# Attention and two gated layers on one core: where the softmax sums of a pair of heads are inverted

## Chip, core and metric

One core of a Trainium2 chip runs the whole program. The metric is device time in microseconds (us), taken on the chip. The kernel before was run three times: 758.63, 758.64 and 758.89 us, median 758.64 us.

## What is computed

The inputs are `q`, `k`, `v` of 2 batches x 8 heads x 1152 positions x 64, and the weights of two gated layers on 1152 tokens of width 512 with 1536 hidden units.

```python
q_pool = q.reshape(B, H, S // 2, 2, D).mean(axis=3)
scores = np.matmul(q_pool, k.transpose(0, 1, 3, 2)) / np.sqrt(D)
attn = np.exp(scores - np.max(scores, axis=-1, keepdims=True))
attn = attn / (np.sum(attn, axis=-1, keepdims=True) + 1e-09)
x = np.matmul(attn, v)                     # then heads side by side: 1152 x 512
xn = x / np.sqrt(np.mean(x * x, -1) + 1e-6) * rms_g
y = (silu(xn @ w_gate) * (xn @ w_val)) @ w_out
out = (sigmoid(y @ w_gate2) * (y @ w_val2)) @ w_out2
```

The part that matters here is the division by the sum of the exponentials plus 1e-9. There are 576 pooled queries per head, so 576 sums per head.

## The kernel before

**Heads in pairs.** The 16 heads are worked through as 8 pairs. Of each head the 576 queries are five chunks of columns (`QCOL`): chunk 0 has 64 queries, chunks 1 to 4 have 128 each. From pair 1 on, chunk 0 of both heads is one block of 128 rows. The scores of a chunk (`s`) come in three matmul groups of 384 keys; VectorE (DVE) copies each out of PSUM with its running maximum (`e,m<-s`), makes the negated maximum `nb` of the three, and ScalarE (ACT) takes the exponential of the chunk, which writes the sum of each row into a column of `sums`. The tensor engine (PE) then transposes the exponentials (`eT`), 128 keys at a time.

**High and low parts.** Each fp32 operand of a product is split into a rounded high part and the rest. For the transposed exponentials `et` ACT writes the high part out of PSUM (line 579) and DVE the low part (line 580). In some units (`POOL_UNITS`) ACT copies the block out (`er`, line 575) and GpSimd (POOL) does both parts (lines 142 and 143, in the function `split`). The products `o` with V follow at a lag of four slots for a DVE unit and of five for a POOL unit (`AV_LAG`).

**Slots.** The order of all engines is written out by hand: `at(g, rank, fn)` puts a step into slot `g`, and a slot's steps are issued by rank, then by the order in which they were registered. Each head has 18 slots: 0 to 8 for the first three query chunks, 9 to 17 for the last two. The scores of a pair begin 15 slots ahead of its first head's slots. Each engine works through its own queue in this order and never past an instruction that waits.

**What sits around the change.** The last exponential of the first head of a pair falls into slot 6 of that head, that of the second head 16 slots on. One slot behind each of them, four after the score unit, `recip` puts two instructions: POOL adds 1e-9 to that head's sums (line 528, 128x5), then DVE takes the reciprocal into `rc` (line 529). When both heads of a pair have their products, the sum `osb` is formed (lines 599, 600), and `o_step` turns it back: PE transposes it (`oT`, line 620), ACT copies it out (`os`, line 631), and POOL multiplies by `rc` (line 629), once for chunks 0 to 2 and once for chunks 3 and 4. The first of these comes some nine slots after the second head's sums.

**Other work in these slots.** POOL also splits the next pair's Q and K (`qq`, `kh`, `kl`) from ACT's copies `kqt`, and V (`vv`). PE transposes K (`kT`, line 339) into the same four PSUM banks (tag "t") that `eT`, `qT` and `oT` use. In the odd heads 1, 3, 5, 9, 11 and 13 a weight block is prepared piece by piece (`w_spread`): ACT lines 208, 216 and 250, DVE lines 228 and 235, POOL lines 236 and 251. After the attention come the two gated layers (lines 741, 840 and 869), which are dense matmuls.

Of the kernel before, what the change touches and what calls it, by code (L numbers as in the profile page):

```python
# [8 lines left out]
F32 = mybir.dt.float32  # L9
# [3 lines left out]
ALU = mybir.AluOpType  # L13
# [3 lines left out]
P = 128  # L17
# [43 lines left out]
def tile_attention_moe_moe(ctx, tc, q, k, v, w_gate1, w_val1, w_out1, rms_g, w_gate2, w_val2, w_out2, out):  # L61
# [3 lines left out]
    nc = tc.nc  # L65
# [13 lines left out]
    NQC = len(QCOL)  # L79
# [12 lines left out]
    def pool(name, side="left", **kw):  # L92
        p = tc.alloc_tile_pool(name=name, bufs=1, side=side, **kw)
        pools.append(p)
        return p
# [9 lines left out]
    ap = pool("ap")  # L105
    ae = pool("ae", side="right")
# [4 lines left out]
    def bank(tag, name):  # L111
        return ps.tile([P, 512], F32, tag=tag, bufs=NBANK[tag], name=name)
# [15 lines left out]
    def at(g, rank, fn):  # L128
        count[0] += 1
        agenda.setdefault(g, []).append((rank, count[0], fn))  # L130
# [163 lines left out]


    kk, qq, vv, esb, osb, tbank = {}, {}, {}, {}, {}, {}
    raw, rcp, xall, sums, eneg, oacc, kst = {}, {}, {}, {}, {}, {}, {}

    SCORES = [[(0, 3), (0, 4), (0, 1), (0, 2), (0, 0)] + [(1, 1), (1, 2), (1, 0), (1, 3), (1, 4)]]
    SCORES += (NP - 1) * [[(0, 1), (0, 2), (0, 0), (0, 3), (0, 4), (1, 1), (1, 2), (1, 3), (1, 4)]]  # L300
# [181 lines left out]
    def s_unit(g, p, k):  # L482

        n, u = divmod(k, NSU)
        j, c = SCORES[p][n]
        i = 2 * p + j
        both = c == 0 and p > 0
        if k == 0:  # L490
            for h in (i, i + 1):
                sums[h] = ap.tile([P, NQC], F32, tag="sums", bufs=4, name="sums")
                esb[h] = {}
                if p == 0:
                    nc.gpsimd.memset(sums[h][QH:P, 0:1], 1.0)
        if u == 0:
            e = ap.tile([P, NSU * SU], F32, tag="e", bufs=8, name="e")
            esb[i][c] = e, 0
            if both:
                esb[i + 1][c] = e, 1  # L500
            eneg[i, c] = (ap.tile([P, NSU], F32, tag="m", bufs=3, name="m"), ap.tile([P, 1], F32, tag="nb", bufs=3, name="nb"))
        e, _ = esb[i][c]
        m, nb = eneg[i, c]
        r = slice(0, P if c or both else QH)
        s = bank("s" if p or k % 4 < 2 else "o", "s")
        kc = slice(u * SU, (u + 1) * SU)
        if both:
            kh, kl = kst[p]
            products = ((qbd[:, 0], kh), (qbd[:, 0], kl), (qbd[:, 1], kh))
        else:  # L510
            products = [(qq[i][:, part, QCOL[c]:QCOL[c] + r.stop], kk[i]) for part in range(2)]
        for n1, (qs, ks) in enumerate(products):
            nc.tensor.matmul(s[r, 0:SU], qs, ks[:, kc], start=(n1 == 0), stop=(n1 == len(products) - 1))  # L513

        def top():

            nc.vector.tensor_scalar(e[r, kc], s[r, 0:SU], 1.0, None, op0=ALU.mult, op1=ALU.max, accum_out=m[r, u:u + 1])  # L517
            if u == NSU - 1:
                nc.vector.tensor_reduce(nb[r], m[r], op=ALU.max, axis=AX.X, negate=True)  # L519

        def swap():
            for h in range(2):
                nc.gpsimd.tensor_copy(sums[i + 1][h * QH:(h + 1) * QH, 0:1], sums[i][(1 - h) * QH:(2 - h) * QH, 0:1])

        def recip():
            if p not in rcp:
                rcp[p] = ae.tile([P, NQC, 2], F32, tag="rc", bufs=2, name="rc")
            nc.gpsimd.tensor_scalar(sums[i], sums[i], 1e-9, 1.0, op0=ALU.add, op1=ALU.mult)
            nc.vector.reciprocal(rcp[p][:, :, j], sums[i])

        at(g, 17, top)
        if u == NSU - 1:
            at(g + EXP_LAG, 12, lambda: nc.scalar.activation(e[r], e[r], AF.Exp, bias=nb[r], scale=1.0, accum_out=sums[i][r, c:c + 1]))  # L533
            if both:
                at(g + 4, 24, swap)
            if n in (4, len(SCORES[p]) - 1):
                at(g + 4, 25, recip)

    def part_of(i, j):
        part, kc = divmod(j, NK)  # L540
# [44 lines left out]
    def av_unit(g, i, part, kc, et):  # L585
        n = NB if part else NA
        if kc == 0:
            oacc[i, part] = bank("o", "o")
        o = oacc[i, part]
        for k in range(2):  # L590
            nc.tensor.matmul(o[:, 0:n], vv[i][:, kc, :], et[:, k, :], start=(kc == 0 and k == 0), stop=(kc == NK - 1 and k == 1))  # L591
        if kc == NK - 1:

            p, odd = divmod(i, 2)
            if p not in osb:
                osb[p] = ae.tile([P, SQ], F32, tag="osb", bufs=1, name="osb")
            r1, r2 = (LP, HP) if odd else (HP, LP)
            ob = osb[p][r1, part * NA:part * NA + n]
            at(g, 11, lambda: nc.scalar.activation(ob, o[r1, 0:n], AF.Copy))
            at(g, 18, lambda: nc.vector.tensor_tensor(ob, o[r2, 0:n], ob, op=ALU.add))  # L600
            g += 1 if i == NHEAD - 1 and part else 2
            if odd:
                at(g, 7, lambda: o_step(g, p, part))

    def o_step(g, p, part):

        b, hp = divmod(p, NPAIR)
        if b not in xall:
            if b == B - 1:
                xa = ae.tile([P, NCA, DM], F32, tag="xa", bufs=1, name="xa")  # L610
                xb = ae.tile([P, NQC - NCA, DM], F32, tag="xb", bufs=1, name="xb")
            else:

                xa, xb = [xpool.tile([P, NDM * (NT - NX0) // DM, DM], F32, tag=f"x{s}1", name="x") for s in "hl"]
            xall[b] = ((xa, 0, NCA), (xb, NCA, NQC))
        x, c0, c1 = xall[b][part]
        n = c1 - c0
        t = bank("t", "oT")
        for c in range(c0, c1):
            nc.tensor.transpose(t[:, (c - c0) * P:(c - c0 + 1) * P], osb[p][:, QCOL[c]:QCOL[c] + P], ident)  # L620
        os = ae.tile([P, 512], F32, tag="kqt", bufs=3, name="os").rearrange("p (c d) -> p c d", d=P)[:, 0:n]
        xs = x[:, 0:n, hp * P:(hp + 1) * P]

        def norm():
            def by_head(t):
                return t.rearrange("p c (j d) -> p c j d", j=2)

            r = rcp[p][:, c0:c1].rearrange("p c (j o) -> p c j o", o=1)
            nc.gpsimd.tensor_tensor(by_head(xs), by_head(os), r.to_broadcast([P, n, 2, D]), op=ALU.mult)

        at(g + 1, 14, lambda: nc.scalar.activation(os.rearrange("p c d -> p (c d)"), t[:, 0:n * P], AF.Copy))
        at(g + 1, 41, norm)
        if hp == NPAIR - 1:
            x_steps(g + 2, b, part)
# [73 lines left out]
    for p in range(NP):  # L708
        for n in range(len(SCORES[p]) * NSU):
            g = 2 * p * NJ + (S0 if p else S00) + n * 2 * NJ // (len(SCORES[p]) * NSU)  # L710
            at(g, 2, lambda g=g, p=p, n=n: s_unit(g, p, n))
    for i in range(NHEAD):
        p, odd = divmod(i, 2)
# [201 lines left out]
```

## Time and profile before

| | us |
|---|---|
| median of three runs | 758.64 |
| the profiled execution's own time | 758.52 |
| its span, first to last instruction | 756.7 |
| PE busy in the span | 733.5 |
| DVE busy | 466.1 |
| ACT busy | 434.8 |
| POOL busy | 396.5 |

The granted TensorE clock is 1.000 over the whole span, which is the 2.4 GHz level. Attention takes about the first 300 us, the gated layers the rest. Matmuls are pipelined, so a row of PE shows from the start of a matmul to its modelled end, and busy time of PE overstates how full it is: what counts is when the next one starts. "Idle before" is time in which an engine did nothing although its queue had work, with what ended it.

### The profile page before, as it was taken

To read this page: it belongs to the slowest core of one execution; us is meant where nothing else is said; L and a number is where in the kernel's file an instruction comes from. 1 tells how busy PE (TensorE), PEld (TensorE's weight loads), DVE (VectorE), ACT (ScalarE), POOL (GpSimd) and SP (SyncE) were. 2 spreads that over 40 slices of the span, in tenths; PEclk is the share of its full clock that TensorE was granted. 3 is DMA by queue.
4 is the path that set the end of the run, shared out by engine and by line. 5 is a ranking of instruction groups with operands and counts; after the bars stand their busy time and mean duration, and the time that the engine had idled before them with its cause. 6 is when DMAs were issued, how large, how long until landed. Compare 5 with 4: busy or idle time off the path is not lost.

```text
span 756.7 us, 12442 instructions
## 1 busy us (share of the span) xinstructions
PE 733.5 (97%) x4501; PEld 690.4 (91%) x4501; DVE 466.1 (62%) x1122; ACT 434.8 (57%) x870; POOL 396.5 (52%) x445
## 2 busy tenths in 40 slices
PE   8999999999999998999999999999999999999997
PEld 6788988888888888999999999999999999998886
DVE  7877878778787888788777664333264456543010
ACT  6787878787888875456555445432354455455000
POOL 6567768677868661166545347442253345347100
PEclk9999999999999999999999999999999999999999
DMA  8536382727273310033332224321222232222011
GB/s 228 132 77 155 82 183 62 182 49 187 63 173 76 95 44 2 2 112 114 109 112 79 63 84 139 111 84 32 81 84 76 68 107 84 84 78 91 0 56 69
DMA packets 68700, 70.23 MB, mean 93 GB/s; under 512 B 19296, under 2 KB 60512, under 8 KB 68640
## 3 DMA queue, kind: packets, MB, share of 16 engines
q1 hardware_dynamic: 68640, 69.45, 33.3%
q8 instruction: 35, 0.57, 0.3%
q14 instruction: 25, 0.20, 0.1%
HBM read 52.63 MB, written 2.36 MB: 73 GB/s over the span
## 4 chain that ended last, share of the span: by engine, by line
PE 75%; POOL 10%; DVE 9%; issue 3%; ACT 3%; POOLq 0%; ACTq 0%
PE acc L741 39%; PE acc L840 10%; PE acc L869 10%; PE o L591 5%; PE s L513 5%; PE eT L354 4%; DVE e L517 4%; DVE et L580 3%; POOL et L143 3%; POOL et L142 1%; POOL kl L143 1%; POOL qq L143 1%; ACT et L579 1%; ACT e L533 1%; POOL w L251 1%
## 5 line engine op out<-in xcount | busy, mean ns | idle before, releaser
L741 PE MATMUL acc<-xh,w 128*128 128x384 f32 (+2 forms) x1184 | 295.5, 331 | 0.4 <-DVE sg L754 0.4
L741 PEld LDWEIGHTS acc<-xh,w 128*128 128x128 f32 x1184 | 211.9, 188 | 0.7 <-DVE sg L754 0.7
L741 PE MATMUL acc<-xl,w 128*128 128x384 f32 (+2 forms) x592 | 195.5, 330 | 0.0
L251 POOL TENSOR_TENSOR w<-wr,w 128x512 fp32r<-128x512 f32 x68 | 99.2, 1458 | 157.7 <-ACT w L250 147.9
L591 PE MATMUL o<-et,vv 128*128 128x256 f32 (+1 forms) x576 | 129.5, 327 | 5.1 <-POOL et L143 2.9
L517 DVE TENSOR_SCALAR_CACHE_REDUCE e<-s 128x384 f32<-128x384 f32 (+1 forms) x219 | 119.4, 553 | 16.6 <-PE s L513 15.0
L236 POOL TENSOR_TENSOR wr<-wsg,wr 128x512 uint32<-128x512 uint32 x72 | 93.9, 1304 | 47.0 <-DVE wsg L235 46.4
L354 PE MATMUL eT<-ident,e 128*128 128x128 f32 (+1 forms) x594 | 112.3, 274 | 0.1
L741 PEld LDWEIGHTS acc<-xl,w 128*128 128x128 f32 x592 | 111.2, 188 | 0.0
L513 PE MATMUL s<-kk,qq 128*128 128x384 f32 (+1 forms) x396 | 109.1, 360 | 1.0 <-DVE kk L422 0.5
L579 ACT ACTIVATE et<-eT 128x512 fp32r<-128x512 f32 (+2 forms) x175 | 84.1, 490 | 35.9 <-PE eT L354 25.0
L580 DVE TENSOR_TENSOR et<-eT,et 128x512 fp32r<-128x512 f32 (+2 forms) x175 | 95.3, 550 | 6.7 <-ACT et L579 5.9
L591 PEld LDWEIGHTS o<-et,vv 128*128 128x128 f32 x576 | 84.8, 190 | 12.0 <-DVE et L580 7.4
L533 ACT ACTIVATE e<-e,nb 128x1152 f32<-128x1152 f32 (+1 forms) x73 | 91.4, 1252 | 1.7 <-DVE nb L519 1.7
L752 ACT ACTIVATE sg<-acc 128x384 f32<-128x384 f32 (+2 forms) x74 | 35.5, 481 | 95.4 <-PE acc L741 95.4
L755 DVE TENSOR_TENSOR sg<-acc,sg 128x384 f32<-128x384 f32 (+2 forms) x74 | 40.5, 547 | 79.8 <-PE acc L741 73.8
L354 PEld LDWEIGHTS eT<-ident,e 128*128 128x128 f32 (+1 forms) x594 | 76.5, 140 | 12.8 <-issue 3.0
L208 ACT ACTIVATE wg<-wraw 128x512 f32<-128x512 f32 x72 | 48.4, 672 | 57.5 <-DVE wsg L235 34.3
L235 DVE SCALAR_TENSOR_TENSOR wsg<-wg,wsg 128x512 uint32<-128x512 uint32 x72 | 79.0, 1097 | 2.3
L840 PE MATMUL acc<-hh,w 128*128 128x384 f32 x288 | 73.2, 334 | 0.0
L513 PEld LDWEIGHTS s<-kk,qq 128*128 128x128 f32 (+1 forms) x396 | 61.1, 187 | 5.3 <-DVE e L517 3.5
L228 DVE TENSOR_SCALAR wsg<-wg 128x512 uint32<-128x512 uint32 x72 | 42.2, 586 | 35.1 <-POOL wr L236 35.0
(114 smaller groups left out, 1019.6 us busy)
## 6 DMA issues: line engine op xcount, KB each, us to landing
wraw<-in_moe_w_gate_dram SPq DMA_DIRECT2D x24, 512.0 KB, 3.5
wraw<-in_moe_w_val_dram SPq DMA_DIRECT2D x24, 512.0 KB, 3.5
wraw<-in_moe_w_out_dram SPq DMA_DIRECT2D x24, 512.0 KB, 3.4
qq<-qq SPq DMA_DIRECT2D x21, 288.0 KB, 3.2
vraw<-in_v_dram SPq DMA_DIRECT2D x16, 288.0 KB, 4.6
kraw<-in_k_dram SPq DMA_DIRECT2D x14, 288.0 KB, 5.0
kk<-kh SPq DMA_DIRECT2D x14, 288.0 KB, 4.2
kk<-kl SPq DMA_DIRECT2D x14, 288.0 KB, 4.8
```

Source lines behind the costliest of these rows:

```text
L235: nc.vector.scalar_tensor_tensor(sg, g, 3, sg, op0=ALU.logical_shift_left, op1=ALU.bitwise_or)
L236: nc.gpsimd.tensor_tensor(r, sg, r, op=ALU.add)
L251: nc.gpsimd.tensor_tensor(t[:, 1], r, t[:, 0].bitcast(F32), op=ALU.subtract)
L354: nc.tensor.transpose(t[:, o:o + r.stop - r.start], x[r], ident[r, r])
L513: nc.tensor.matmul(s[r, 0:SU], qs, ks[:, kc], start=(n1 == 0), stop=(n1 == len(products) - 1))
L517: nc.vector.tensor_scalar(e[r, kc], s[r, 0:SU], 1.0, None, op0=ALU.mult, op1=ALU.max, accum_out=m[r, u:u + 1])
L533: at(g + EXP_LAG, 12, lambda: nc.scalar.activation(e[r], e[r], AF.Exp, bias=nb[r], scale=1.0, accum_out=sums[i][r, c:c + 1]))
L579: at(g, 12, lambda: nc.scalar.activation(hi, t, AF.Copy))
L580: at(g + 1, 20, lambda: nc.vector.tensor_tensor(lo, t, hi.bitcast(F32), op=ALU.subtract))
L591: nc.tensor.matmul(o[:, 0:n], vv[i][:, kc, :], et[:, k, :], start=(kc == 0 and k == 0), stop=(kc == NK - 1 and k == 1))
L741: nc.tensor.matmul(acc[:, 0:nt], wt[:, ws, dc * P:(dc + 1) * P], xs[:, dc], start=(dc == 0 and n == 0), stop=(dc == NDM - 1 and n == 2))
L840: nc.tensor.matmul(acc[t][:, 0:NTT], w[:, ws, (fc % 4) * P:(fc % 4 + 1) * P], hs[fc][:, cs], start=(fc == 0 and n == 0), stop=(fc == NFC - ...
```

## The change

`sums` of both heads become the halves of one tile of 128x2x5. Behind the last exponential of the second head POOL adds 1e-9 to the whole tile at once (`add_small`). Behind the first head nothing is issued any more. The reciprocal of the whole tile is taken by DVE in the slot in which `o_step` transposes the first part of `osb`, and is written with heads and chunks swapped into the same `rc`.

```diff
         if k == 0:
+            both_sums[p] = ap.tile([P, 2, NQC], F32, tag="sums", bufs=2, name="sums")
             for h in (i, i + 1):
-                sums[h] = ap.tile([P, NQC], F32, tag="sums", bufs=4, name="sums")
+                sums[h] = both_sums[p][:, h - i]
...
-        def recip():
-            if p not in rcp:
-                rcp[p] = ae.tile([P, NQC, 2], F32, tag="rc", bufs=2, name="rc")
-            nc.gpsimd.tensor_scalar(sums[i], sums[i], 1e-9, 1.0, op0=ALU.add, op1=ALU.mult)
-            nc.vector.reciprocal(rcp[p][:, :, j], sums[i])
+        def add_small():
+            nc.gpsimd.tensor_scalar(both_sums[p], both_sums[p], 1e-9, 1.0, op0=ALU.add, op1=ALU.mult)
...
-            if n in (4, len(SCORES[p]) - 1):
-                at(g + 4, 25, recip)
+            if n == len(SCORES[p]) - 1:
+                at(g + 4, 25, add_small)
...
     def o_step(g, p, part):
         b, hp = divmod(p, NPAIR)
+        if not part:
+            rcp[p] = ae.tile([P, NQC, 2], F32, tag="rc", bufs=2, name="rc")
+            at(g, 18, lambda: nc.vector.reciprocal(rcp[p].rearrange("p c j -> p j c"), both_sums[p]))
```

DVE's queue behind the last scores of the first head of a pair, before (`e,m<-s`: scores out of PSUM; `et`: low part of the transposed exponentials):

```order
L517 TENSOR_SCALAR e,m<-s 128x384
L519 TENSOR_REDUCE nb<-m 128x1
L529 RECIPROCAL rc<-sums 128x5
L580 TENSOR_TENSOR et<-eT,et 128x320
L517 TENSOR_SCALAR e,m<-s 128x384
L580 TENSOR_TENSOR et<-eT,et 128x320
```

and with the change:

```order
L518 TENSOR_SCALAR e,m<-s 128x384
L520 TENSOR_REDUCE nb<-m 128x1
L578 TENSOR_TENSOR et<-eT,et 128x320
L518 TENSOR_SCALAR e,m<-s 128x384
L578 TENSOR_TENSOR et<-eT,et 128x320
```

The reciprocal is gone and `et` stands directly behind the maximum; behind the second head the same instruction goes in the same way.

DVE's queue some nine slots after the second head's sums, where that pair is turned back (`osb`: its out^T), with the change:

```order
L598 TENSOR_TENSOR osb<-o,osb 64x320
L578 TENSOR_TENSOR et<-eT,et 128x512
L518 TENSOR_SCALAR e,m<-s 128x384
L608 RECIPROCAL rc<-sums 128x2x5
L578 TENSOR_TENSOR et<-eT,et 128x512
L518 TENSOR_SCALAR e,m<-s 128x384 x2
```

Before, the same rows stood there without the reciprocal; it now stands between a score copy and an `et`.

POOL's queue at the first head's sums, before (`er`: ACT's copy of `eT`; `kqt`: its copy of `kT`):

```order
L142 TENSOR_SCALAR et<-er 128x320
L143 TENSOR_TENSOR et<-er,et 128x320
L528 TENSOR_SCALAR sums<-sums 128x5
L142 TENSOR_SCALAR kh<-kqt 128x512
L143 TENSOR_TENSOR kl<-kqt,kh 128x512
```

With the change the row of line 528 is gone here; at the second head's sums it stays at its place and reads 128x10. The queues of PE, ACT and SyncE are unchanged, and no DMA is moved.

## Rows read from the trace of the kernel before

**Rows 1.** Busy us of each engine (x instructions) in a stretch: attention, then gated layers.

```profile
160.00:200.00 40.00, 37.71 (x274) 34.84 (x273) 31.77 (x102) 33.20 (x70) 31.20 (x46) 1.00 0.46 112
340.00:500.00 160.00, 160.00 (x925) 160.00 (x924) 99.42 (x153) 81.30 (x154) 81.85 (x60) 1.00 0.32 99
```

**Rows 2.** Waits, whole span: who waited for whom, us in total, times, longest.

```profile
DVE rc L529 <- POOL sums L528: 28.5, 14, 2.8
...
PE kT L339 <- DVE et L580: 8.1, 6, 1.4
PE o L591 <- POOL et L143: 2.9, 4, 0.7
```

**Rows 3.** Waits of PE's weight loads, 60 to 271 us, columns as in rows 2.

```profile
PEld o L591 <- DVE et L580: 5.0, 20, 0.3
...
PEld s L513 <- DVE e L517: 2.7, 12, 0.3
```

**Rows 4.** Lines 528 and 529: count, ns min/median/max, first and last start.

```profile
L528 POOL TENSOR_SCALAR sums<-sums x16: 197/199/202, 20.5 to 290.0; 128x5 f32<-128x5 f32 x16
L529 DVE RECIPROCAL rc<-sums x16: 181/191/192, 20.8 to 290.6; 128x5 f32<-128x5 f32 x16
```

**Rows 5.** Timeline of DVE, pair 2, first head: start, duration, idle before.

```profile
98.91 0.19 DVE L529 RECIPROCAL rc<-sums 128x5 f32<-128x5 f32 x1 [2.80 <-POOL sums L528]
99.01 0.45 DVE L580 TENSOR_TENSOR et<-eT,et 128x320 fp32r<-128x320 f32 x1
```

**Rows 6.** Timeline of POOL, same place.

```profile
97.73 0.86 POOL L143 TENSOR_TENSOR et<-er,et 128x320 fp32r<-128x320 f32 x1
98.67 0.20 POOL L528 TENSOR_SCALAR sums<-sums 128x5 f32<-128x5 f32 x1
```

**Rows 7.** Timeline of ACT, same place.

```profile
95.68 0.44 ACT L579 ACTIVATE et<-eT 128x320 fp32r<-128x320 f32 x1
```

**Rows 8.** Timeline of PE, same place.

```profile
97.78 0.38 PE L354 MATMUL eT<-ident,e 128*128 128x128 f32 x2
99.52 0.33 PE L339 MATMUL kT<-ident,kraw 128*128 128x128 f32 x1 [1.36 <-DVE et L580]
99.60 0.83 PE L591 MATMUL o<-et,vv 128*128 128x320 f32 x4
100.28 0.51 PE L513 MATMUL s<-kk,qq 128*128 128x384 f32 x2
```

**Rows 9.** Timeline of DVE and PE, pair 1, second head.

```profile
78.21 0.19 DVE L529 RECIPROCAL rc<-sums 128x5 f32<-128x5 f32 x1 [1.45 <-POOL sums L528]
...
79.30 0.30 PEld L513 LDWEIGHTS s<-kk,qq 128*128 128x128 f32 x2 [0.28 <-DVE e L517]
```

**Rows 10.** Timeline of POOL, pair 2, second head, with the idle time ahead of it.

```profile
108.39 0.46 POOL L142 TENSOR_SCALAR et<-er 128x320 fp32r<-128x320 f32 x1 [4.46 <-ACT er L575]
...
113.30 1.29 POOL L251 TENSOR_TENSOR w<-wr,w 128x512 fp32r<-128x512 f32 x1
...
115.10 1.11 POOL L143 TENSOR_TENSOR et<-er,et 128x320 fp32r<-128x320 f32 x1
```

**Rows 11.** Timeline of DVE, same place.

```profile
115.08 0.42 DVE L228 TENSOR_SCALAR wsg<-wg 128x512 uint32<-128x512 uint32 x1
```

**Rows 12.** Timeline of PE, same place.

```profile
116.26 0.71 PE L591 MATMUL o<-et,vv 128*128 128x320 f32 x3 [0.73 <-POOL et L143]
```

**Rows 13.** Timelines of POOL and PE, pair 7, first head.

```profile
275.49 0.20 POOL L528 TENSOR_SCALAR sums<-sums 128x5 f32<-128x5 f32 x1
...
279.94 0.66 PE L668 MATMUL xT<-ident,x 128*128 128x128 f32 x4 [0.77 <-POOL x L663]
```

**Rows 14.** Timelines of DVE, ACT and POOL where the reciprocal of pair 2 goes.

```profile
121.70 0.69 DVE L580 TENSOR_TENSOR et<-eT,et 128x512 fp32r<-128x512 f32 x1
...
123.14 0.48 ACT L631 ACTIVATE os<-oT 128x384 f32<-128x384 f32 x1
...
123.70 0.83 POOL L629 TENSOR_TENSOR x<-os,rc 128x384 f32<-128x384 f32 x1 [0.72 <-ACT os L631]
```

More of the change, by code (lines that the diff above doesn't have):

```diff
@@ L296, in tile_attention_moe_moe @@
     kk, qq, vv, esb, osb, tbank = {}, {}, {}, {}, {}, {}
-    raw, rcp, xall, sums, eneg, oacc, kst = {}, {}, {}, {}, {}, {}, {}
+    raw, rcp, xall, sums, both_sums, eneg, oacc, kst = {}, {}, {}, {}, {}, {}, {}, {}
     SCORES = [[(0, 3), (0, 4), (0, 1), (0, 2), (0, 0)] + [(1, 1), (1, 2), (1, 0), (1, 3), (1, 4)]]
```

## The prediction

> **What bounds the kernel now.** I read the windows by stage first. In the gated layers PE is busy 160.00 of 160 us; in attention 37.71 of 40, while DVE, ACT and POOL are each busy 31 to 33 of 40 [rows 1]. So the layers are set by PE alone and this change, which touches only attention, can do nothing there; attention is a chain through four engines in which none is full, and a wait on any of them can reach PE.
>
> Second, the waits. DVE's reciprocal waited for POOL's addition 14 times, 28.5 us in total, up to 2.8 [rows 2]. The reader is to see that this is a queue standing still: behind the reciprocal lie the low parts and the score copies that PE needs. It is not yet a cost, since DVE has idle time. The cost is what PE waited in turn: `kT` for DVE's `et` 6 times, 8.1 us, 1.35 each [rows 2]. That is the longest wait of PE, and it is tied to the reciprocal in the timelines: DVE idles 2.80 us, takes the reciprocal at 98.91 and the low part at 99.01, and at 99.52 `kT` starts after 1.36 us of idling on just that `et` [rows 5, 8]. `kT` needs a PSUM bank that this `et` had not yet read out. ACT's high part of the same block was done at 95.68 + 0.44 = 96.12 [rows 7], so the low part stood some 2.9 us in the queue for nothing but the addition.
>
> Why was the addition late? POOL put it behind a long split that ended at 97.73 + 0.86 = 98.59 [rows 6]. POOL was not waiting, it was working through its queue. This matters below: removing the reciprocal does not make POOL any earlier.
>
> **The first head of pairs 1 to 6.** The change takes both instructions away here. DVE can do the low part from about 96.1, so the bank is free before `kT` could start, which is behind the transposes of 97.78 [rows 8]. PE then comes at about 98.1 to the four `o` products that stood at 99.60. Two of these belong to a POOL unit (lag five), two to a DVE unit (lag four); the POOL unit was registered first. Its high part is there; its low part is the split that ends at 98.59 [rows 6]. So the second of the four starts at 98.59. The four took 100.28 - 99.60 = 0.68 until the next scores, 0.17 each [rows 8]; three after 98.59 put the scores at 99.10 instead of 100.28. That is **1.18 us** per pair, and less than the 1.36 that PE idled, because POOL is next in line. Six pairs: 6 x 1.18 = 7.1 us. What follows in DVE's queue (a score copy, the maximum, the next `et`) hangs on those scores and shifts by the same amount, so I count no further gain from DVE's freed 2.8 us.
>
> **The second head.** Here DVE's stop is shorter, 1.45 us, and PE's scores wait 0.28 for a DVE copy [rows 9]. In pairs 1 and 3 nothing else is late, so I take 2 x 0.28 = 0.6. In pairs 2, 4, 5 and 6 a weight block is prepared at the same time, and PE stops soon after for POOL's split, 4 times, 2.9 us [rows 2]: in pair 2 that split ends at 115.10 + 1.11 = 116.21, and PE goes on at 116.26 [rows 10, 12]. POOL's addition stays here, so what PE gains ahead of 116.26 it waits there: nothing gained. Pair 0 had a stop too, without a PE wait: nothing.
>
> **Pair 7** has its first head next to the last normalisation of batch 0. PE's stop at 279.94 is for POOL, and POOL's queue gets shorter by the one addition of 0.20 [rows 13]: 0.2 us.
>
> **What is added.** Eight reciprocals of 128x10 in the place of 16 of 128x5 (191 ns [rows 4]); no row shows the larger one, and its output is strided. Its cost lies between nothing, if DVE has room where it goes, and 8 x 0.19 = 1.5 us if DVE's queue there is what PE waits for. I take nothing: the same instruction leaves an equally full stretch of that queue, twice. POOL's addition of 128x10 replaces one of 128x5 (0.20 us), eight fewer in all. The reciprocal now waits for an addition that POOL made some nine slots earlier, so nothing queues up behind it. POOL's multiplication at 123.70 waited 0.72 us for ACT's `os`, which ended at 123.14 + 0.48 = 123.62; the reciprocal would come in behind the `et` of 121.70 or just ahead of it [rows 14], over a microsecond before. PE's, ACT's and SyncE's queues are unchanged, no DMA is moved.
>
> **The sum.** 7.1 + 0.6 + 0.2 = 7.9 us off the profiled execution's 758.52: **750.7**. The median of the runs shown is 758.64, 0.12 higher, which is 0.02% and is left out. Bounds: if POOL did not gate the first heads, 8.1 in place of 7.1; if POOL's split at 115.10 lost the excess over the 0.86 that a split of this size takes [rows 6], 4 x 0.25 = 1.0 more; on the other side 1.5 for the reciprocals and 1.7 for the weight pairs (next part). That spans 748.5 to 753.9.
>
> **Rivals.**
>
> *The weight pairs lose (752.4).* With DVE about 1 us earlier there, its line 228 (0.42 us, at 115.08) would be issued while POOL is in line 251, which ends at 113.30 + 1.29 = 114.59, or just ahead of POOL's next split. Before, it began just ahead of the split of 115.10, which took 1.11 where 0.86 is usual [rows 6, 10, 11]: the two get in each other's way. If POOL then waits out all of line 228 on its way to the split that PE stands for, that is 4 x 0.42 = 1.7 us back: 750.7 + 1.7 = 752.4. The Trainium skill ("SBUF — State Buffer", Who interferes with whom) says it more sharply: DVE and GpSimd share one pair of SBUF ports, and the instruction that comes second is blocked until the first has ended. By that rule line 228 costs POOL its whole 0.42 us if it is first; this trace agrees in kind, with 0.25 lost. Against this rival: if POOL comes first, DVE waits instead, and DVE now has time there.
>
> *POOL does not move with PE (755.4).* In the four weight pairs POOL's split at 116.21 would stay where it is and PE would wait off the 1.18 gained half a pair earlier. Then only pairs 1 and 3 keep theirs: 2 x 1.18 + 0.6 + 0.2 = 3.1. Against it: POOL idled 4.46 us before 108.39 for a copy of ACT's, which follows PE's transposes [rows 10], so POOL starts that stretch when PE lets it.
>
> *DVE's debt is paid off as well (742.7 at the furthest).* PE's weight loads waited for `et` and score copies 5.0 + 2.7 us between 60 and 271 us [rows 3], many of them just behind a stop. If all of that went, with the full 8.1: 758.5 - 15.8 = 742.7. Against it: those steps hang on PE's own scores, as said.
>
> *No effect (758.5).* DVE had slack anyway, and the bank of `kT` or ACT's queue is late for another reason. Against it: the wait's end at 99.52 follows the `et` of 99.01.
>
> *Slower (762.6).* POOL's multiplication now depends on a DVE instruction that stands in a full stretch of DVE's queue; POOL takes its work in order, and behind the multiplication lie the splits of the next pair's Q and K. If DVE came there later than ACT's `os`, every pair would lose the difference. That decides from some 1.7 us of lateness on (121.9 against 123.62); at 1.5 us beyond that point 8 x 1.5 = 12 is lost against 7.9 won: 762.6. For it: that stretch of DVE is dense. Against it: the multiplication already idles 0.72 us, and DVE is earlier than before, not later.
>
> **How the numbers follow.** Forecast 0.58; weight pairs lose 0.12; POOL does not move 0.10; debt paid off 0.08; no effect 0.06; slower 0.06. The predicted time is the forecast's, 750.7, its own range 748.5 to 753.9. The range of 746.5 to 755.5 takes in the second rival and part of the fourth and leaves out the rest. A measurement of this kernel can tell about 0.2%, 1.5 us, from no change; of these cases all but the last two are faster by more: 0.88, the same 0.06, slower 0.06.
>
> **What would show it.** DVE's 28.5 us of waiting for `sums` gone and no wait of POOL or DVE for `rc` in its place; `kT`'s six waits gone from PE's list, and in their place about 0.5 us before the second `o` product, put down to POOL's split; the four waits for POOL's split beside the weights still there, longer by about 0.3 each; from the end of attention on the same rows, about 8 us earlier. The prediction is wrong if `kT` still waits, if PE's waits for POOL grow by more than 3 us in total, or if POOL is seen waiting for the new reciprocal.

## The result and the profile after

The changed kernel takes **750.85 us** (median of 4 runs, 750.73 to 750.86), the kernel before on the same chip 758.66 (4 runs). The ratio is 0.9896, with a 95% interval of 0.9879 to 0.9913, which makes it faster by more than the 0.2% that can be told from no change. The forecast was 750.7.

The waits of the changed kernel over the whole span (who waited for whom, us in total, times, longest):

```profile
DVE e L518 <- PE s L514: 28.6, 55, 0.9
...
PE o L589 <- POOL et L143: 3.7, 10, 0.5
...
PE o L589 <- POOL et L142: 1.6, 4, 0.5
```

DVE's 28.5 us for `sums` and PE's six waits of `kT` [rows 2] have no row any more. DVE's busy time rose a little, from 466.1 us to 470.9, and it now idles for PE's scores, 28.6 us where it was 15.0 before. PE's stops for POOL's split grew from 2.9 us [rows 2] to 3.7 + 1.6 = 5.3. The moved reciprocal, by its tile (ns minimum/median/maximum, first and last start in us):

```profile
L608 DVE RECIPROCAL rc<-sums x8: 207/212/213, 50.9 to 288.3; 128x10 f32<-128x10 f32 x8
```

Twice the columns cost 212 ns instead of 191 [rows 4]. The two stretches of [rows 1]:

```profile
160.00:200.00 40.00, 38.52 (x277) 35.49 (x275) 33.72 (x106) 33.98 (x71) 32.63 (x47) 1.00 0.54 127
...
340.00:500.00 160.00, 160.00 (x925) 160.00 (x924) 94.13 (x146) 79.55 (x149) 81.30 (x59) 1.00 0.31 96
```

In attention every engine is denser; the layers issue the same 925 matmuls in 160 us. Their first and last products, by the tile `acc`, of the kernel before:

```profile
L741 PE MATMUL acc<-xh,w x1184: 272/334/402, 299.4 to 678.9; 128*128 128x384 f32 x182, 128*128 128x288 f32 x11, 128*128 128x192 f32 x5
...
L869 PE MATMUL acc<-wl,hh x72: 388/389/389, 722.6 to 752.3; 128*128 128x512 f32 x72
```

and of the changed kernel:

```profile
L742 PE MATMUL acc<-xh,w x1184: 272/334/402, 291.5 to 671.0; 128*128 128x384 f32 x182, 128*128 128x288 f32 x11, 128*128 128x192 f32 x5
...
L870 PE MATMUL acc<-wl,hh x72: 388/389/389, 714.8 to 744.4; 128*128 128x512 f32 x72
```

The layers begin 7.9 us earlier and end 7.9 us earlier: the whole gain was made in attention.

**Pair 2, first head.** Timelines of DVE, POOL and PE at the place of [rows 5, 6, 8] (start, us, engine, line):

```profile
94.45 0.16 DVE L520 TENSOR_REDUCE nb<-m 128x1 f32<-128x3 f32 x1
94.65 0.49 DVE L578 TENSOR_TENSOR et<-eT,et 128x320 fp32r<-128x320 f32 x1
95.88 0.56 DVE L518 TENSOR_SCALAR_CACHE_REDUCE e<-s 128x384 f32<-128x384 f32 x1 [0.74 <-PE s L514]
...
96.22 0.88 POOL L143 TENSOR_TENSOR et<-er,et 128x320 fp32r<-128x320 f32 x1
...
96.25 0.38 PE L354 MATMUL eT<-ident,e 128*128 128x128 f32 x2
96.47 0.27 PE L339 MATMUL kT<-ident,kraw 128*128 128x128 f32 x1
96.50 0.39 PE L589 MATMUL o<-et,vv 128*128 128x320 f32 x1
97.15 0.71 PE L589 MATMUL o<-et,vv 128*128 128x320 f32 x3 [0.26 <-POOL et L143]
97.70 0.51 PE L514 MATMUL s<-kk,qq 128*128 128x384 f32 x2
```

`et` follows the maximum at once and `kT` waits for nothing. PE then stands between the first `o` and the other three until POOL's split has ended (96.22 + 0.88 = 97.10), as the prediction had it. From `kT` to the next scores it is 1.23 us; it was 100.28 - 99.52 = 0.76 before [rows 8]. So by the next scores 0.47 of what `kT` gained is given back to POOL. From the last transposes ahead of `kT` to those scores it took 100.28 - 97.78 = 2.50 us before [rows 8] and takes 97.70 - 96.25 = 1.45 now: this head gains 1.05.

**Pair 2, second head, beside a weight block**, POOL, DVE and PE, at the place of [rows 10 to 12]:

```profile
110.74 1.30 POOL L251 TENSOR_TENSOR w<-wr,w 128x512 fp32r<-128x512 f32 x1
112.02 0.63 POOL L142 TENSOR_SCALAR et<-er 128x320 fp32r<-128x320 f32 x1
112.73 0.86 POOL L143 TENSOR_TENSOR et<-er,et 128x320 fp32r<-128x320 f32 x1
...
111.64 0.68 DVE L228 TENSOR_SCALAR wsg<-wg 128x512 uint32<-128x512 uint32 x1
...
112.91 1.23 DVE L235 SCALAR_TENSOR_TENSOR wsg<-wg,wsg 128x512 uint32<-128x512 uint32 x1
...
112.70 0.41 PE L589 MATMUL o<-et,vv 128*128 128x320 f32 x1 [0.28 <-POOL et L142]
113.64 0.71 PE L589 MATMUL o<-et,vv 128*128 128x320 f32 x3 [0.53 <-POOL et L143]
```

DVE's line 228 now begins while POOL is in line 251 (110.74 + 1.30 = 112.04) and takes 0.68 instead of 0.42 [rows 11]; POOL's split keeps its 0.86. PE's one stop of 0.73 [rows 12] has become two, 0.28 + 0.53 = 0.81. In pair 5 (and in pair 6) line 228 takes longer still; DVE and POOL:

```profile
214.37 0.92 DVE L228 TENSOR_SCALAR wsg<-wg 128x512 uint32<-128x512 uint32 x1
...
213.72 1.30 POOL L251 TENSOR_TENSOR w<-wr,w 128x512 fp32r<-128x512 f32 x1
```

In pair 2 as in pair 5 it ends 0.27 to 0.28 behind line 251: 112.32 against 112.04, and 215.29 against 215.02.

**Where the reciprocal went**, DVE, ACT and POOL at the place of [rows 14]:

```profile
119.08 0.21 DVE L608 RECIPROCAL rc<-sums 128x10 f32<-128x10 f32 x1
...
120.51 0.48 ACT L632 ACTIVATE os<-oT 128x384 f32<-128x384 f32 x1
...
121.08 0.83 POOL L630 TENSOR_TENSOR x<-os,rc 128x384 f32<-128x384 f32 x1 [0.73 <-DVE nb L520]
```

It is done 1.79 us before the multiplication begins, which still idles 0.73 (0.72 before). The row puts that down to a DVE instruction, but ACT's `os` ends at 120.51 + 0.48 = 120.99, just ahead of the multiplication, as before. In the other pairs the reciprocal is done 1.79 us ahead as well, but for 1.66 in pair 6 and 0.62 in pair 7, and there too `os` ends last: the reciprocal gates nobody.

### The profile page after: what moved, and what is told of

Its sections match the earlier page's. It is cut to its first block, busy times and chain, and to the rows that moved or that the text cites. A ratio compares the mean times of both kernels' runs of the same rounds, so it can differ in the third digit from the quotient of the medians.

```text
span 748.9 us, 12425 instructions
## 1 busy us (share of the span) xinstructions
PE 731.4 (98%) x4501; PEld 690.1 (92%) x4501; DVE 470.9 (63%) x1114; ACT 434.0 (58%) x870; POOL 394.9 (53%) x437
## 4 chain that ended last, share of the span: by engine, by line
PE 78%; POOL 9%; DVE 8%; ACT 2%; issue 2%; DMA 0%; POOLq 0%; ACTq 0%
PE acc L742 39%; PE acc L841 10%; PE acc L870 10%; PE o L589 6%; PE s L514 5%; PE eT L354 5%; DVE e L518 3%; POOL et L143 2%; DVE et L578 2%; POOL et L142 1%; POOL kl L143 1%; POOL qq L143 1%; PE eT L563 1%; POOL w L251 1%; ACT et L577 1%
## 5 line engine op out<-in xcount | busy, mean ns | idle before, releaser
L518 DVE TENSOR_SCALAR_CACHE_REDUCE e<-s 128x384 f32<-128x384 f32 (+1 forms) x219 | 120.1, 554 | 31.3 <-PE s L514 28.6
L235 DVE SCALAR_TENSOR_TENSOR wsg<-wg,wsg 128x512 uint32<-128x512 uint32 x72 | 81.2, 1127 | 2.3
L228 DVE TENSOR_SCALAR wsg<-wg 128x512 uint32<-128x512 uint32 x72 | 43.8, 609 | 35.1 <-POOL wr L236 35.0
```

The source lines that it names most:

```text
L235: nc.vector.scalar_tensor_tensor(sg, g, 3, sg, op0=ALU.logical_shift_left, op1=ALU.bitwise_or)
```

## Experiments

Theory: the reciprocal of a first head held DVE's queue until POOL had come to its addition; `kT` and the scores paid; POOL's split is next in line, and what DVE does in its freed time is hidden. In the expectations of e1 to e5, rival A says that having fewer instructions is what saves, and rival B that every microsecond of DVE's standing still costs alike. A third, here rival C, came up only with e1: how DVE and POOL meet beside the weight blocks decides part of it. The later expectations name their own rivals.

Diffs are against the changed kernel unless said otherwise, and `...` marks lines left out; in e1 to e5 these give each head its own `sums` tile again and split `recip` from the addition. Ratios are to the kernel before, run beside each experiment (758.55 to 758.64 us). A step of PE is what it gains or loses from one matmul to the next, worked out from the starts of the same matmuls in two traces.

**e1: only the first head's reciprocal is moved**, to just behind the second's; sums and additions stay per head.

```diff
...
-            if n == len(SCORES[p]) - 1:
+            if n in (4, len(SCORES[p]) - 1):
                 at(g + 4, 25, add_small)
+            if n == len(SCORES[p]) - 1:
+                at(g + 4, 26, lambda: recip(1))
+                at(g + 4, 27, lambda: recip(0))
...
-            at(g, 18, lambda: nc.vector.reciprocal(rcp[p].rearrange("p c j -> p j c"), both_sums[p]))
```

> All 16 additions and 16 reciprocals stay; only the first head's reciprocal moves, to directly behind the second head's. Theory (the gain is the first head's stop of DVE, which PE feels through the PSUM bank of kT, and POOL is next in line there): 6 x 1.18 = 7.1 us of the 7.8 come, 751.5 us, kT's six waits gone, the second heads' waits of about 1.5 us still there. Rival A (fewer instructions make the gain): none are saved, so 758.6. Rival B (every microsecond of DVE's standing still costs alike): the first heads hold 18.7 of the 28.5 us, so 66% of 7.8 us, 753.5.

Measured: 753.06 us (752.86 to 753.13), ratio 0.9928 [0.9913, 0.9942]. That is 1.6 us more than the theory said, and close to rival B's 753.5. `kT` waits no longer, and by the steps the first heads give 1.05 to 1.10 us each. But in each of the four weight pairs PE loses 0.45 to 0.47 at the scores and the `oT` behind line 228, and makes up for about half of it by a shorter stop for POOL's split: 0.17 to 0.25 lost on balance. DVE and POOL, pair 2:

```profile
112.85 1.10 DVE L228 TENSOR_SCALAR wsg<-wg 128x512 uint32<-128x512 uint32 x1
...
112.80 0.86 POOL L143 TENSOR_TENSOR et<-er,et 128x320 fp32r<-128x320 f32 x1
```

Line 228 begins 0.05 us behind POOL's split, and ends 0.29 behind it: 1.10 instead of 0.42, the split its usual 0.86. Score copies behind it come late, and PE's scores with them. So rival C, which the theory had left out, has a share here; e1 alone does not tell it from rival B, e5 and e2 do.

**e2: only the second head's reciprocal is moved**, to where the change takes it; the first head's stays.

```diff
...
-            if n == len(SCORES[p]) - 1:
+            if n in (4, len(SCORES[p]) - 1):
                 at(g + 4, 25, add_small)
+            if n == 4:
+                at(g + 4, 26, lambda: recip(0))
...
-            at(g, 18, lambda: nc.vector.reciprocal(rcp[p].rearrange("p c j -> p j c"), both_sums[p]))
+            at(g, 18, lambda: nc.vector.reciprocal(rcp[p][:, :, 1], sums[2 * p + 1]))
```

> The complement: only the second head's reciprocal moves, to where out^T is turned back; the first head's stays where it was. Theory: pairs 1 and 3 win 0.3 each and the weight pairs nothing, so 758.0 us, with kT's six waits of 1.35 us still there. Rival A: 758.6, nothing is saved. Rival B: 34% of 7.8 us, 756.0.

Measured: 757.08 (756.91 to 757.2), ratio 0.998 [0.997, 0.9989]. Waits:

```profile
DVE rc L531 <- POOL sums L526: 18.6, 7, 2.8
...
PE kT L339 <- DVE et L584: 8.0, 6, 1.4
```

`kT`'s waits are all there: they belong to the first heads. The second heads alone give 1.5 us: by steps some 0.5 in pair 1 and in pair 3, and 0.1 or less in each weight pair. The result lies midway between the theory's 758.0 and rival B's 756.0.

**e3: the work is not merged.** 16 additions at their old places, two reciprocals of 128x5 where the change has one.

```diff
...
-            if n == len(SCORES[p]) - 1:
+            if n in (4, len(SCORES[p]) - 1):
                 at(g + 4, 25, add_small)
...
-            at(g, 18, lambda: nc.vector.reciprocal(rcp[p].rearrange("p c j -> p j c"), both_sums[p]))
+            for h in range(2):
+                at(g, 18, lambda h=h: nc.vector.reciprocal(rcp[p][:, :, h], sums[2 * p + h]))
```

> All 16 additions stay where they were, one per head; both reciprocals, one per head, go where out^T is turned back. Nothing is merged, only DVE's wait is gone. Theory: the same as the change but for the addition of 0.2 us that pair 7's POOL chain keeps, 751.1 us. Rival A (merging): 758.6, or at least 2 us over the change.

Measured: 750.54 (750.41 to 750.73), ratio 0.9895 [0.9878, 0.9911]. Rival A falls: with as many instructions as before it is as fast as the change, to within 0.2%. What counts is the place of the reciprocals.

**e4: the kernel before, with the first head's addition a slot earlier on POOL** and the reciprocal where it was (diff against the kernel before).

```diff
...
-            if n in (4, len(SCORES[p]) - 1):
-                at(g + 4, 25, recip)
+            if n == 4:
+                at(g + 3, 40, add_small)
+                at(g + 4, 25, lambda: recip(0))
+            if n == len(SCORES[p]) - 1:
+                at(g + 4, 25, add_small)
+                at(g + 4, 25, lambda: recip(1))
```

> The kernel before, with the first head's addition a slot earlier in POOL's queue, ahead of the multiplication and of the split that it stood behind. DVE still waits for it, in the same place. Theory: the wait falls from 2.8 to about 0.8 us, DVE is in time for kT, and the split behind the addition ends about 0.28 us later, at which PE now stands: 6 x 0.9 = 5.4 us won, 753.2. Rival A: 758.6, no instruction is saved. If a wait on DVE's queue costs at any length, more than 754.5.

Measured: 754.43 (753.98 to 755.78), ratio 0.9949 [0.9934, 0.9964]. This shortens the wait without moving the reciprocal, and gains 4.1 of the change's 7.8 us, where the theory said 5.4. DVE's waits for `sums` fall to 14.6 us, and `kT` waits no longer. PE, by steps, wins 1.45 to 1.54 per first head and keeps 0.67 to 0.70 of it (0.9 was expected), since the addition now stands ahead of POOL's split; its waits for the split:

```profile
PE o L597 <- POOL et L143: 6.1, 10, 0.7
```

So what stood in the queue behind the reciprocal was the cause, and POOL's split is the next limit. The time alone would not say so: 754.43 is just short of the 754.5 that was expected if a wait cost at any length.

**e5: only the first head's reciprocal is moved, to where the change takes it.**

```diff
...
-            if n == len(SCORES[p]) - 1:
+            if n in (4, len(SCORES[p]) - 1):
                 at(g + 4, 25, add_small)
+            if n == len(SCORES[p]) - 1:
+                at(g + 4, 26, lambda: recip(1))
...
-            at(g, 18, lambda: nc.vector.reciprocal(rcp[p].rearrange("p c j -> p j c"), both_sums[p]))
+            at(g, 18, lambda: nc.vector.reciprocal(rcp[p][:, :, 0], sums[2 * p]))
```

> Like the run in which only the first head's reciprocal moved (753.06), but it goes where out^T is turned back, so that DVE's queue behind the second head's sums is that of the kernel before, with one reciprocal and its wait. Theory: that run lost 0.46 us in each of the four weight pairs because DVE came 0.1 us later to line 228, just behind POOL's split instead of just ahead of it, and was shut out for 0.7 us. Here line 228 stands ahead of the split again (0.42 us, the split 1.11), and the first heads show their full 6 x 1.18: 751.5. Rival B (each microsecond of DVE's standing still costs alike): as in that run, 753 to 753.5.

Measured: 752.05 (751.84 to 753.1), ratio 0.9916 [0.9901, 0.9931]. It lies 1.0 us below e1, from which only the place of one reciprocal differs; line 228 begins 0.02 us ahead of POOL's split here and takes 0.42, as in [rows 10, 11], and the weight pairs lose nothing. DVE's wait:

```profile
DVE rc L531 <- POOL sums L526: 9.8, 7, 1.6
```

With e2 this answers rival B. Here 28.5 - 9.8 = 18.7 us of waiting behind the first heads went, for 6.6 us of time (0.35 us for each); in e2 28.5 - 18.6 = 9.9 us behind the second heads, for 1.5 (0.15 each). They do not cost alike. But the theory's 751.5 was missed too, by 0.55: by the steps a first head gives 1.03 to 1.06 us and not 1.18.

**e6: the changed kernel with 16 reciprocals of 128x5 that wait for nothing**, at the places where the removed ones stood. They read a new tile of ones in the constants; nothing uses their result.

```diff
     nc.gpsimd.memset(nhalf, -0.5)
+    ones = const.tile([P, 5], F32, name="ones")
+    nc.gpsimd.memset(ones, 1.0)
...
+            if n in (4, len(SCORES[p]) - 1):
+                at(g + 4, 26, lambda: nc.vector.reciprocal(ae.tile([P, NQC], F32, tag="free", bufs=2, name="free"), ones))
```

> The changed kernel, with 16 reciprocals of 128x5 added in DVE's queue where the old ones stood; they read a tile of ones and wait for nobody. Their results are not used. Theory: DVE idles 0.7 to 0.9 us behind each of these places, so the instruction costs nothing there, 751.0 us, at most 751.5. Rival A (the number of instructions made the gain): 16 x 0.19 = 3.0 us back, 753.9.

Measured: 755.53 (755.44 to 755.59), ratio 0.9957 [0.9943, 0.9971], 4.7 us above the change. Both expectations missed. The first layer begins at 291.8, only 0.3 later than in the changed kernel; 4.5 us are lost in the layers, where no instruction was added (windows, columns as above):

```profile
340.00:500.00 160.00, 160.00 (x917) 160.00 (x916) 94.54 (x147) 78.80 (x148) 79.56 (x58) 1.00 0.31 96
```

917 matmuls in the place of 925. That called for e9, e11 and e12, which came after e7 and e8.

**e9: the same reciprocals without the new tile**; they read `nhalf`, which is there anyway.

```diff
+            if n in (4, len(SCORES[p]) - 1):
+                at(g + 4, 26, lambda: nc.vector.reciprocal(ae.tile([P, NQC], F32, tag="free", bufs=2, name="free"), nhalf.to_broadcast([P, NQC])))
```

> The changed kernel with sixteen more reciprocals that wait for nothing, as in e6, but they read a tile that is there anyway, so no tile is added in front of the others. Theory (the reciprocal's own 0.2 us is hidden, and e6's loss came from the added tile): 751.0, at most 751.5, and the matmuls of the gated layers stand 173.2 ns apart as in the changed kernel. Rival A (the added VectorE work costs the time): 753.9 or more, as e6 had it in all but the layers, with the layers again 175 ns apart.

Measured: 750.52 (750.41 to 750.76), ratio 0.9895 [0.988, 0.9909]. Sixteen reciprocals in the old places cost nothing when they do not wait:

```profile
L537 DVE RECIPROCAL free<-nhalf 128x5 f32<-128x5 f32 x16 | 2.9, 180 | 0.0
...
340.00:500.00 160.00, 160.00 (x925) 160.00 (x924) 94.17 (x146) 79.52 (x149) 81.21 (x59) 1.00 0.29 96
```

So the wait was the price, not the 2.9 us of work (the group's columns: busy us, mean ns, idle before).

**e11 and e12: the changed kernel with an unused tile in the constants**, of 20 and of 64 bytes per partition (`[P, 5]` and `[P, 16]`), written once. The diff of e11:

```diff
+    ones = const.tile([P, 5], F32, name="ones")
+    nc.gpsimd.memset(ones, 1.0)
```

> The changed kernel with one tile of 128x5 floats (20 bytes of a partition) more in the constants, written once and never read, and nothing else. Theory (e6's loss in the layers comes from where the tiles lie): about 755.2, with the matmuls of the layers 175 ns apart. Rival (it came from the added reciprocals): 750.9.

> As e11, with a tile of 128x16 floats (64 bytes of a partition). If any shift of the tiles costs: about 755, as e11. If only a shift that leaves the tiles on other offsets within a line of 64 bytes does: 750.9, with the layers at 173.2 ns.

Measured: e11 755.28 (755.14 to 755.35), ratio 0.9957 [0.9942, 0.9972]; e12 751.86 (751.77 to 751.97), ratio 0.9912 [0.9896, 0.9929]. The tile alone costs what e6 lost. The last layer's products by the tile `acc`, of e11:

```profile
L872 PE MATMUL acc<-w,hh x144: 388/394/397, 674.6 to 746.4; 128*128 128x512 f32 x144
...
L872 PE MATMUL acc<-wl,hh x72: 389/396/398, 718.8 to 749.1; 128*128 128x512 f32 x72
```

and of e12:

```profile
L872 PE MATMUL acc<-w,hh x144: 388/393/398, 671.4 to 742.8; 128*128 128x512 f32 x144
...
L872 PE MATMUL acc<-wl,hh x72: 388/389/392, 715.6 to 745.5; 128*128 128x512 f32 x72
```

In the changed kernel it is 389 for `wl,hh`, start to start 226.7 ns between the `w,hh` products; in e11 396 and 230.2, in e12 389 and 230.0. Of e12's two expectations neither is quite right: 64 bytes cost 1.0 us, 20 bytes 4.4.

**e7: POOL's normalisation of part 1 a slot later**, so that the split that PE waits for comes first (not in the last pair of a batch).

```diff
-        at(g + 1, 41, norm)
+        at(g + 1 + (part and hp < NPAIR - 1), 41, norm)
```

> The changed kernel, with POOL's second multiplication of a pair a slot later for the first three pairs of each batch, so that it stands behind the split that PE waits for in the next pair's first head, not ahead of it. Theory (POOL's split is what stands next in line): PE's wait there of about 0.5 us goes in pairs 1, 2, 3, 5 and 6 (2.2 to 2.6 us), and 0.3 in pair 7: 748.2 us. If another engine stands next: 750.9.

Measured: 748.10 (748.02 to 748.4), ratio 0.9862 [0.9847, 0.9876]. PE in pair 2:

```profile
95.81 0.27 PE L339 MATMUL kT<-ident,kraw 128*128 128x128 f32 x1
95.83 0.84 PE L589 MATMUL o<-et,vv 128*128 128x320 f32 x4
96.51 0.51 PE L514 MATMUL s<-kk,qq 128*128 128x384 f32 x2
```

All four `o` products run through, and `kT` to scores takes 0.70 instead of 1.23. POOL's split was the next in line.

**e8: the weights' last casts (line 251) four slots later.**

```diff
-W_SLOTS = (6, 8, 9, 13, 13)
+W_SLOTS = (10, 8, 9, 13, 13)
```

> The changed kernel, with the last step of a weight block (ACT line 250, POOL line 251, 1.3 us) in slot 10 of its head instead of slot 6, behind the splits that PE waits for. Theory: PE's waits of 0.28 + 0.53 us (0.5 + 0.5 in pairs 5 and 6) for POOL in the four weight pairs go, some 4 x 1.1 = 4.4 us with what is hidden in the weight loads, less up to 4 x 0.4 because DVE's line 228 now meets the split instead: 747.0 us, between 746 and 749. If POOL's port and not its queue is what PE waits for there: 750.9.

Measured: 748.04 (747.85 to 748.07), ratio 0.986 [0.9845, 0.9874]. Against the changed kernel PE gains 1.3 to 1.4 at each weight pair (in pair 2 all four `o` products run through from 112.22 on, where they stood at 112.70 and 113.64 above), but gives half of it back where DVE and POOL meet anew. Line 228 by its tile in attention:

```profile
L228 DVE TENSOR_SCALAR wsg<-wg x5: 794/810/1039, 78.2 to 246.4; 128x512 uint32<-128x512 uint32 x5
```

It takes nearly twice its 0.42 at least, and behind pair 6 PE loses 0.85 in one place, where it waits for a score copy of DVE.

**e10: e7 and e8 together.**

> The changed kernel with POOL's norm of part 1 a slot later (e7) and the weights' casts a slot later (e8) together. Theory (the two take away different waits of PE, 2.75 and 2.8 us): 745.3, between 745 and 746. Rival (they act on the same waits at the weight pairs): 747 to 748, no better than either.

Measured: **744.17** (744.02 to 745.11), ratio 0.9813 [0.9798, 0.9828] to the kernel before, and 6.7 us below the change; 745 to 746 was expected. That is 1.1 more than the two single gains make (2.75 + 2.81 = 5.56); most of it is the 0.85 that e8 lost behind pair 6, which does not occur here. PE's waits for POOL's split are gone but for one:

```profile
PE o L589 <- POOL et L143: 0.2, 1, 0.2
```

It is the best version found.

## Why the prediction was right

The mechanism was right. That the time came within 0.2 us of the forecast is in part luck: the largest term was 0.8 us too high, two others together 0.9 too low.

**The first heads: right in kind, a little too high.** Six times 1.18 = 7.1 was forecast. By PE's steps each gains 1.5 to 1.6 at `kT` and the first `o`, gives 0.47 to 0.54 back at the second and third, and keeps 1.03 to 1.05: 6.3 together, the same in e5. The 0.13 between is in the last part of the working, which put the scores three times 0.17 behind the end of POOL's split. That split ended 97.10 - 96.25 = 0.85 us behind the last transposes (98.59 - 97.78 = 0.81 before), PE began again 0.05 behind it, and the three products took 97.70 - 97.15 = 0.55 and not 0.51. e2 shows that `kT`'s waits belong to these heads, e4 that it was the wait and the queue behind it, e7 that POOL's split was the next limit.

**The second heads: mis-sized.** "2 x 0.28 = 0.6" for pairs 1 and 3 and "nothing gained" in the weight pairs were low. In the change pairs 1 and 3 give 0.52 and 0.44 and the weight pairs 0.05 to 0.10 each, some 1.3 together; alone, in e2, they brought 1.5 us of time. The step that failed is to count the 0.28 by which one weight load waited: the scores behind it move by 0.30 + 0.11 us, and in pair 1 `oT` adds 0.10.

**Pair 7: mis-sized.** 0.2 was forecast for a shorter POOL queue; PE gains 0.39 there. It does come from that queue: e3 and e5, which keep the addition, gain 0.02. But the addition cost POOL more than its own 0.20, with the gaps around it. POOL before, then with the change:

```profile
274.53 0.88 POOL L143 TENSOR_TENSOR et<-er,et 128x320 fp32r<-128x320 f32 x1
275.49 0.20 POOL L528 TENSOR_SCALAR sums<-sums 128x5 f32<-128x5 f32 x1
275.79 0.69 POOL L662 TENSOR_SCALAR x<-x,ss 128x512 f32<-128x512 f32 x1
```

```profile
267.03 0.88 POOL L143 TENSOR_TENSOR et<-er,et 128x320 fp32r<-128x320 f32 x1
267.89 0.70 POOL L663 TENSOR_SCALAR x<-x,ss 128x512 f32<-128x512 f32 x1
```

From one start to the other it is 1.26 before and 0.86 now, 0.40 less. The sum, 6.3 + 1.3 + 0.4 = 8.0, agrees with the 7.9 us by which the layers begin earlier. In the forecast's range the lower bound should read 748.7 (750.7 - 1.0 - 1.0), not 748.5; nothing hangs on it.

**The added reciprocal: right.** No cost beside 8 x 0.21 us of work (e3 and e9 show that neither the number nor the size matters), and no wait for `rc`, so the slower rival has nothing to stand on.

**The weight pairs: the rival's mechanism occurred, but its price did not.** Line 228 does come under line 251, as the rival had it, yet DVE pays for it with 0.68 instead of 0.42 (0.92 in pair 5), while POOL loses 0.63 - 0.46 = 0.17 on the short instruction behind [rows 10]. By the steps PE gives back 0.34 in pair 2 at the `o` products, and had gained 0.41 just ahead. In e1 line 228 fell behind the split instead, and the pairs lost some 0.2 each on balance. The Trainium skill ("SBUF — State Buffer", Who interferes with whom) says that where a DVE instruction uses the SBUF ports that DVE and GpSimd share, the second one is blocked until the first has ended. Where POOL came first the traces agree: in e1 the split kept 0.86 and line 228 ended 0.29 behind it, and beside line 251 it ended 0.27 to 0.28 behind. [rows 10, 11] agree only in kind: line 228 came first with its 0.42, and the split lost 0.25. Which of them is first changes with a tenth of a microsecond, so a loss in the weight pairs was a fair rival, and it is not excluded for a neighbouring edit: e1 is one, at about half the rival's 0.42 a pair.

**The other rivals fell.** POOL moved with PE: the weight pairs kept what their first heads had gained. Of DVE's debt little was paid: the weight loads' waits in the whole span fell from 7.4 to 6.2 us for `et` and from 3.5 to 1.5 for score copies.

**What was to be seen** came as written, but for two numbers: the weight pairs' stops grew by 0.2 each in place of 0.3 ((1.6 + 4 x 0.53 - 2.9) / 4), and the idle time before the second `o` product shows as 0.26 in pair 2, in place of 0.5 (by the starts the second and third lose 0.54). PE's waits for POOL grew by 2.4 us at the split and by 0.5 elsewhere (`xT` from 1.1 to 1.4, `qT` from 0.7 to 0.9): 2.9, just under the 3 that would have made the prediction wrong.

## What to carry to other kernels

An instruction of 0.19 us cost 1.05 us, over five times its length, because it was issued where its input was not ready: the price of such an instruction is what stands behind it in its engine's queue and is needed by the bottleneck. Move such a step to the place of its use, and before costing the gain find the next engine in line; its queue then shows the next edit, as e7 and e8 did. When a probe adds a tile, measure the tile alone as well.

## What the hardware showed that was not expected

An unused tile of 20 bytes per partition in the constants makes the dense layers 4.5 us slower: from the first to the last `acc` product it is 749.1 - 291.7 = 457.4 us in e11 and 744.4 - 291.5 = 452.9 in the changed kernel, at a granted clock of 1.00 in both. With 64 bytes it is 745.5 - 291.5 = 454.0. The products themselves stand further apart: in e11 175.1 ns instead of 173.3 between the `xh,w` products of 384 columns (mean, start to start). With 64 bytes most of the loss, 0.8 of 1.1 us, falls in the last layer: its `w,hh` products stand nearly as far apart as in e11, while those of 384 columns keep 173.5. e11 and e12 issue the same instructions and differ in the tile's size alone, so the difference between them is not the added instruction. What the size changes is where the tiles placed behind this one lie in SBUF, which is the likely cause; that was argued, not shown, and which tile's place matters stays open. The change itself is free of it: its `sums` take 2 x 40 bytes in the place of 4 x 20, and its layers take as long as before.
